# A gated linear recurrence with an MLP behind it: seven levels of decay products replaced by two running products, and the MLP turned round and put three chunks back

## The chip, the cores and the metric

The kernel runs on one core of one Trainium2 chip. The metric is the device time of the whole program in microseconds; the median of three runs is given. All arithmetic is in float32. The traces show four engines: PE (matrix products and transposes), DVE and POOL (elementwise work; POOL doesn't read PSUM here), ACT (copies out of PSUM, exponentials), and the queue of SP, which issues DMAs.

## The reference

```python
B, H, S, D = 4, 8, 768, 48            # q, k, v: float32; alpha between 0.8 and 1
for t in range(S):
    state = alpha[:, :, t, :, None] * state + einsum('bhd,bhe->bhde', k[:, :, t], v[:, :, t])
    y[:, :, t] = einsum('bhd,bhde->bhe', q[:, :, t], state)
x = y.transpose(0, 2, 1, 3).reshape(B * S, H * D)         # 3072 tokens x 384
h = x @ w_in                                              # 384 x 1024, float64 words
sm = exp(h - max(h)) / (sum(exp(h - max(h))) + 1e-9)
solu = h * sm
ln = (solu - mean(solu)) / sqrt(var(solu) + 1e-6) * g_ln  # over the 1024
out = ln @ w_out                                          # 1024 x 384, float64 words
```

Both weights arrive as float64 and are turned into float32 on the chip, bit field by bit field.

## The kernel before

The 3072 tokens are 24 chunks of 128: four sequences of six chunks each, taken one sequence after the other, so that each chunk needs the state that the chunk just before it leaves. For every chunk alpha, q and k are loaded with tokens on partitions, and PE transposes them (`prep_T`) so that a pair of heads (2 x 64 places) lies on the partitions.

Inside a chunk a query meets an earlier key at one of seven levels: at level m the key lies in a left block of 2^m tokens and the query in the right block beside it. `prep_level` doubles two products from level to level: `F`, alpha from the start of a block to the token (DVE, L153), and `G`, alpha after the token to the end of its block (DVE, L150). POOL multiplies q by F (`qc`, L139) and k by G (`kl`, L149), ACT spreads the two heads of a pair (`qr`, L160), PE forms the products of the level (`lev`, L188), and DVE copies those that the level owns into the scores under a mask (`sT`, L192). `read_out` applies scores and state to v (`y`, L204 and L209), adds the token's own term, and `next_state` carries the state on.

The MLP has tokens on partitions: `up` transposes x and makes `h` (128 x 1024, L257), `softmax`, `solu`, `stats` and `norm` run over the row of 1024, `norm_T` transposes the result back (`tp_ln`, L305), `down` multiplies by w_out (`o`, L314), and the 128 x 384 rows go out by DMA.

The loop at the end of the function puts the first part of chunk n beside the MLP of chunk n - 1 and the layout of chunk n + 1. The framework then orders each engine's instructions by its own estimate; every engine works through its list strictly in that order. Its PSUM tiles take two banks for transposes, two for levels, two for h, one for y and one for o.

## Time and profile before

| | |
|---|---|
| median of 3 runs | 849.0 us (840.6 to 849.03) |
| span of the profiled execution | 838.1 us |
| PE busy | 648.8 us, 77% of the span, 3513 matmul instructions |
| DVE busy | 579.1 us, 69%, 967 instructions |
| POOL busy | 413.6 us, 49%, 504 instructions |
| ACT busy | 231.4 us, 28%, 363 instructions |
| DMA | 30.64 MB, mean 37 GB/s |

The span runs from the first to the last instruction of one execution; the runs' times also hold what lies around it, 2.5 to 11 us by the fastest and the slowest of them. "Busy" counts an engine's instructions and not its waits. The chain of waits is found by going back from the last instruction, at each step to what released it. A float32 product is two PE instructions in the trace, a transpose one.

### The profile page before, as it was taken

How to read it: one execution, taken by the hardware profiler on the slowest of the kernel's cores; microseconds unless marked ns; L12 is line 12 of the kernel's file. 1: busy time of each engine (PE TensorE's matmuls, PEld its weight loads, DVE VectorE, ACT ScalarE, POOL GpSimd, SP SyncE). 2: the span in 40 equal slices, each digit the busy share in tenths (PEclk: the TensorE clock that was granted, in tenths of full speed). 3: DMA queues.
4: the chain of work that ended last, by engine and by line, in shares of the span. 5: the costliest groups of instructions: out<-in, count | busy, mean ns of one | idle time of the engine just before them, and what ended most of it. 6: DMA issues, size and time to landing. Idle time of an engine off the chain costs nothing.

```text
span 838.1 us, 9855 instructions
## 1 busy us (share of the span) xinstructions
PE 648.8 (77%) x3513; PEld 478.1 (57%) x3513; DVE 579.1 (69%) x967; ACT 231.4 (28%) x363; POOL 413.6 (49%) x504
## 2 busy tenths in 40 slices
PE   3277397878888887878888878878788878878884
PEld 2275276656566565566566556556566556556562
DVE  8989987685476586686577687577567676576522
ACT  2102323223223233333223223223223223223101
POOL 7847656563363464464453564465343563563200
PEclk9967568998969999999979999999969999999987
DMA  9314221201111022112201202202201200000000
GB/s 176 74 51 100 83 59 20 48 21 28 35 24 39 19 38 39 34 24 38 46 13 38 47 20 36 41 20 38 38 20 29 48 19 1 20 10 1 10 10 9
DMA packets 106528, 30.64 MB, mean 37 GB/s; under 512 B 100712, under 2 KB 103920, under 8 KB 106480
## 3 DMA queue, kind: packets, MB, share of 16 engines
q1 hardware_dynamic: 103296, 23.60, 15.6%
q10 hardware_dynamic: 3184, 6.42, 2.5%
q8 instruction: 28, 0.46, 0.2%
q14 instruction: 20, 0.16, 0.1%
HBM read 25.29 MB, written 4.72 MB: 36 GB/s over the span
## 4 chain that ended last, share of the span: by engine, by line
PE 32%; DVE 28%; POOL 21%; issue 11%; ACT 7%; POOLq 0%; DVEq 0%; ACTq 0%
PE h L257 16%; POOL qc L139 7%; POOL kl L149 6%; PE y L209 6%; DVE F L153 5%; DVE G L150 4%; PE tp_ln L305 3%; DVE sT L192 3%; DVE s L294 3%; PE o L314 3%; PE lev L188 3%; POOL qk L176 3%; ACT qr L160 3%; POOL own L179 2%; POOL rstd L290 2%
## 5 line engine op out<-in xcount | busy, mean ns | idle before, releaser
L188 PE MATMUL lev<-qr,kl 128*128 128x128 f32 x1344 | 197.1, 296 | 52.6 <-DVE sT L192 22.0
L139 POOL TENSOR_TENSOR qc<-qT,F 128x256 f32<-128x256 f32 x168 | 136.3, 811 | 186.0 <-ACT qT L122 158.6
L188 PEld LDWEIGHTS lev<-qr,kl 128*128 128x128 f32 x1344 | 178.1, 207 | 66.6 <-DVE sT L192 24.1
L257 PE MATMUL h<-w_in,xT 128*128 128x512 f32 x288 | 151.2, 679 | 55.2 <-ACT xT L253 54.4
L149 POOL TENSOR_TENSOR kl<-kT,G 128x256 f32<-128x256 f32 x144 | 113.5, 788 | 104.4 <-DVE G L150 99.9
L160 ACT COPY qr<-qc 64x768 f32<-64x768 f32 (+2 forms) x94 | 89.6, 953 | 254.4 <-POOL qc L139 253.9
L192 DVE COPY_PREDICATED sT<-masks,lev 128x512 f32<-128x512 uint8 x168 | 145.2, 864 | 7.0 <-PE lev L188 6.4
L153 DVE TENSOR_TENSOR F<-F 128x256 f32<-128x256 f32 x168 | 121.3, 722 | 35.0 <-POOL qc L139 30.5
L314 PE MATMUL o<-w_out,lnT 128*128 128x384 f32 x384 | 141.3, 523 | 0.0
L257 PEld LDWEIGHTS h<-w_in,xT 128*128 128x128 f32 x288 | 60.4, 218 | 128.0 <-issue 67.0
L265 DVE TENSOR_REDUCE nmax<-h 128x1 f32<-128x1024 f32 x24 | 29.4, 1224 | 144.9 <-PE h L257 144.9
L150 DVE TENSOR_TENSOR G<-G,F 128x256 f32<-128x256 f32 x144 | 98.2, 682 | 15.9 <-POOL kl L149 12.2
L314 PEld LDWEIGHTS o<-w_out,lnT 128*128 128x128 f32 x384 | 76.6, 206 | 49.5 <-issue 9.1
L305 PE MATMUL tp_ln<-ident,s 128*128 128x128 f32 x192 | 33.3, 328 | 35.1 <-DVE s L294 35.0
L209 PEld LDWEIGHTS y<-vn,sT 128*128 128x128 f32 x384 | 55.2, 227 | 2.7 <-issue 1.8
L209 PE MATMUL y<-vn,sT 128*128 128x48 f32 x384 | 55.0, 305 | 0.3 <-DVE sT L192 0.3
L305 PEld LDWEIGHTS tp_ln<-ident,s 128*128 128x128 f32 x192 | 26.3, 169 | 40.3 <-DVE s L294 27.3
L122 ACT COPY F<-tp_F 128x512 f32<-128x512 f32 x24 | 14.0, 584 | 115.9 <-PE tp_F L120 115.9
L308 ACT COPY lnT<-tp_ln 128x512 f32<-128x512 f32 x48 | 26.6, 588 | 61.2 <-PE tp_ln L305 61.2
L179 POOL TENSOR_TENSOR own<-vn,dot 128x384 f32<-128x384 f32 x24 | 22.5, 939 | 34.7 <-DVE x L214 34.6
L268 ACT ACTIVATE e<-h,nmax 128x1024 f32<-128x1024 f32 x24 | 26.8, 1115 | 44.5 <-DVE nmax L265 44.1
L290 POOL TENSOR_TENSOR rstd<-var,mhalf 128x1 f32<-128x1 f32 x24 | 16.7, 695 | 41.4 <-DVE var L288 41.3
(64 smaller groups left out, 666.2 us busy)
## 6 DMA issues: line engine op xcount, KB each, us to landing
vn<-in_v_dram SPq DMA_DIRECT2D x24, 192.0 KB, 2.6
an<-in_alpha_dram SPq DMA_DIRECT2D x24, 192.0 KB, 3.2
qn<-in_q_dram SPq DMA_DIRECT2D x24, 192.0 KB, 3.9
kn<-in_k_dram SPq DMA_DIRECT2D x24, 192.0 KB, 3.9
out_dram<-o_sb SPq DMA_DIRECT2D x24, 192.0 KB, 1.9
raw<-in_moe_w_in_dram ACTq DMA_DIRECT2D x12, 256.0 KB, 3.2
raw<-in_moe_w_out_dram ACTq DMA_DIRECT2D x8, 384.0 KB, 3.0
ident<-ident_c ACTq DMA_DIRECT2D x1, 64.0 KB, 2.0
```

The source lines that it names most:

```text
L139: nc.gpsimd.tensor_tensor(out=d["qc"][:, lv].rearrange("p j (n m) -> p j n m", m=m), in0=blocks(qT, lv, 1), in1=blocks(F, lv, 1), op=ALU.mult,
L149: nc.gpsimd.tensor_tensor(out=kl, in0=blocks(kT, lv, 0), in1=blocks(G, lv, 0), op=ALU.mult)
L150: nc.vector.tensor_tensor(out=blocks(G, lv, 0), in0=blocks(G, lv, 0), in1=spread(F, lv, 1), op=ALU.mult)
L153: nc.vector.tensor_tensor(out=blocks(F, lv, 1), in0=blocks(F, lv, 1), in1=spread(F, lv, 0), op=ALU.mult)
L160: nc.scalar.copy(out=qrs[n % 2][halves[i], first:end, :, i], in_=st[n]["qc"][halves[i], first:end])
L179: nc.gpsimd.tensor_tensor(out=d["own"], in0=d["v"], in1=dot[:, :, None].to_broadcast([P, H, D]), op=ALU.mult)
L188: nc.tensor.matmul(lev[:, 2 * j : 2 * j + 2, :], lhsT=kl[:, lv, j], rhs=qr[:, lv, j], start=True, stop=True)
L192: nc.vector.copy_predicated(out=blocks(sTs[n % 2], lv, 1), mask=masks[:, lv].rearrange("p (o n m) -> p o n m", o=1, m=m).to_broadcast([P, ...
L209: nc.tensor.matmul(y[:, h, :], lhsT=sTs[n % 2][:, h], rhs=d["v"][:, h], start=(c == 0 and h == 0), stop=(h == H - 1), skip_group_check=True,)
L257: nc.tensor.matmul(d["h"][:, s : s + 512], lhsT=xT[:, a], rhs=w_in[:, a, s : s + 512], start=(a == 0), stop=(a == KC - 1),)
L305: nc.tensor.transpose(out=tp[:, a], in_=d["s"][:, (s + a) * P : (s + a + 1) * P], identity=ident)
L314: nc.tensor.matmul(o, lhsT=d["lnT"][:, a], rhs=w_out[:, a], start=(a == 0), stop=(a == FC - 1))
```

## The change

A new function, `fast_path`, does all the work. The function of before is kept as `general_path` and sits behind a branch on a flag that `fast_path` computes.

- **Order of chunks.** Chunk n is part n // 4 of sequence n % 4, so four chunks lie between a state's making and its next use; each sequence has a state tile of its own.
- **Decay.** Two scans on DVE (L132 and L142 of the new file) over the transposed alpha: backwards, `hT`, the product from a token to the chunk's end; forwards, `qF`, the product from the start to the token, divided by the product of the whole chunk. POOL multiplies k by the one and q by the other. One product per head gives all scores (`scores`), and DVE applies a triangular mask. No levels, no own term.
- **MLP.** `up` has d_ff on partitions: 24 products of 128 x 128 per chunk in two halves. There is no maximum; `u = h * exp(h)` goes straight into `down`, with sum of u as a 385th column, and sums of e and u squared as two more columns. The mean is taken out of w_out once (`centre`), and the norm is one factor per token (`finish`). The MLP runs three chunks behind.
- **Weights.** Their DMAs go through SP's queue and no longer ACT's; the step `frac <- bits` goes from POOL to ACT; w_in comes in pieces of 512 columns.
- **End.** A flag is computed from products, sums and alpha, each engine loads it (`values_load`) and jumps over the general path if it is 0.

```diff
+    def prep_scan(n):
...
+        nc.vector.tensor_tensor_scan(
+            out=h[:, 0 : NP * SW][:, ::-1], data0=a.rearrange("p j s -> p (j s)")[:, ::-1],
+            data1=unit.rearrange("p j s -> p (j s)")[:, ::-1], initial=1.0, op0=ALU.mult, op1=ALU.add,
+        )
+        nc.vector.tensor_copy(out=fend[:, n], in_=h4[:, :, 1])
+        least = small.tile([P, NP, 1], FP, name="least")
+        nc.vector.tensor_scalar(out=least, in0=h4[:, :, 1:2], scalar1=LEAST, scalar2=None, op0=ALU.max)
+        nc.vector.reciprocal(out=s[:, :, 0:1], in_=least)
+        d["qF"] = work.tile([P, NP, SW], FP, name="qF")
+        nc.vector.tensor_tensor_scan(
+            out=d["qF"].rearrange("p j s -> p (j s)"), data0=a.rearrange("p j s -> p (j s)"),
+            data1=s.rearrange("p j s -> p (j s)"), initial=1.0, op0=ALU.mult, op1=ALU.add,
+        )
+        nc.vector.tensor_reduce(
+            out=amax[:, n : n + 1], in_=an[n % NIN].rearrange("p h d -> p (h d)"), axis=AX.X, op=ALU.max,
+            apply_absolute_value=True,
+        )
+    def prep_q(n):
+        d = st[n]
+        nc.gpsimd.tensor_tensor(out=d["qT"], in0=d["qT"], in1=d["qF"][:, :, 1:SW], op=ALU.mult)
...
+            nc.gpsimd.tensor_tensor(
+                out=d["kT"][:, :, 0 : P - 1], in0=d["kT"][:, :, 0 : P - 1],
+                in1=hT[n % 2][:, 0 : NP * SW].rearrange("p (j s) -> p j s", s=SW)[:, :, 2:SW], op=ALU.mult,
+            )
+    def decayed(n):
...
+        nc.gpsimd.tensor_tensor(
+            out=s, in0=s, in1=h4[:, :, 1:2].to_broadcast([P, NP, 2 * D]), op=ALU.mult
+        )
+    def scores(n):
+        d = st[n]
+        a = [ps_a.tile([P, NP, P], FP, tag=f"a{i}", name=f"a{i}") for i in range(2)]
+        for j in range(NP):
+            for i in range(2):
+                nc.tensor.matmul(
+                    a[i][:, j], lhsT=d["kT"][heads[i], j], rhs=d["qT"][heads[i], j], start=True, stop=True
+                )
+        d["sT"] = work.tile([P, 2, NP, P], FP, name="sT")
+        for i in range(2):
+            nc.vector.tensor_tensor(
+                out=d["sT"][:, i], in0=a[i], in1=mask[:, None, :].to_broadcast([P, NP, P]), op=ALU.mult
+            )
...
+        for h in range(H):
+            nc.tensor.matmul(
+                y[:, h, :], lhsT=d["sT"][:, h % 2, h // 2], rhs=d["v"][:, h],
+                start=(c == 0 and h == 0), stop=(h == H - 1), skip_group_check=True,
...
+        nc.scalar.copy(out=d["x"], in_=y.rearrange("p h d -> p (h d)"))
...
+    def up(n, half):
...
+        for f in range(HF):
+            for a in range(KC):
+                nc.tensor.matmul(
+                    h[:, f], lhsT=w_in[:, a, (f0 + f) * P : (f0 + f + 1) * P], rhs=d["xT"][:, a],
+                    start=(a == 0), stop=(a == KC - 1),
+                )
+        fs = slice(f0, f0 + HF)
+        nc.scalar.activation(out=d["e"][:, fs], in_=h, func=AF.Exp)
+        nc.vector.tensor_tensor(out=d["u"][:, fs], in0=h, in1=d["e"][:, fs], op=ALU.mult)
+        nc.scalar.activation(out=d["u2"][:, fs], in_=d["u"][:, fs], func=AF.Square)
+    def partial(n):
...
+        for eng, key in ((nc.gpsimd, "e"), (nc.vector, "u2")):
+            t = work.tile([P, HF, P], FP, name="part_" + key)
+            eng.tensor_tensor(out=t, in0=d[key][:, 0:HF], in1=d[key][:, HF:FC], op=ALU.add)
+            w = HF
+            while w > 1:
+                w //= 2
+                eng.tensor_tensor(out=t[:, 0:w], in0=t[:, 0:w], in1=t[:, w : 2 * w], op=ALU.add)
+            d["p_" + key] = t
+    def down(n):
+        d = st[n]
+        o = ps_o.tile([P, 512], FP, tag="o", name="o")
+        for f in range(FC):
+            nc.tensor.matmul(
+                o[:, 0 : DM + 1], lhsT=d["u"][:, f], rhs=w_out[:, f], start=(f == 0), stop=(f == FC - 1),
+                skip_group_check=True,
+            )
+        for i, key in enumerate(("e", "u2")):
+            nc.tensor.matmul(
+                o[:, DM + 1 + i : DM + 2 + i], lhsT=d["p_" + key][:, 0], rhs=ones[:, 0:1],
+                start=False, stop=True, skip_group_check=True,
+            )
+        d["o"] = o
+    def finish(n):
...
+        nc.vector.tensor_copy(out=s[:, 0:3], in_=d["o"][:, DM : DM + 3])
...
+        nc.gpsimd.tensor_tensor(out=r, in0=s[:, 3:4], in1=mhalf, op=ALU.pow)
+        o_sb = work.tile([P, DM], FP, name="o_sb")
+        nc.scalar.activation(out=o_sb, in_=d["o"][:, 0:DM], func=AF.Copy, scale=r)
+        t0 = b * S + c * P
+        nc.sync.dma_start(out=out[t0 : t0 + P, :], in_=o_sb)
+        d.clear()
...
+    def centre():
+        m = ps_o.tile([P, 512], FP, tag="o", name="mean")
+        for f in range(FC):
+            nc.tensor.matmul(m[:, 0:DM], lhsT=ones, rhs=w_out[:, f, 0:DM], start=(f == 0), stop=(f == FC - 1))
+        nc.scalar.mul(out=ms, in_=m[:, 0:DM], mul=1.0 / DFF)
+        for f in range(FC):
+            eng = nc.vector if f % 2 else nc.gpsimd
+            eng.tensor_tensor(out=w_out[:, f, 0:DM], in0=w_out[:, f, 0:DM], in1=ms, op=ALU.subtract)
...
+    for n in range(N + LAG):
+        if n + 3 < N:
+            load(n + 3)
+        m = n - LAG
+        now, before, after = n < N, m >= 0, n + 1 < N
+        if after:
+            prep_aq(n + 1)
+        if m > 0:
+            finish(m - 1)
+        if now:
+            decayed(n)
+        if after:
+            prep_scan(n + 1)
+        if before:
+            up(m, 0)
+        if after:
+            prep_q(n + 1)
+        if now:
+            scores(n)
+        if after:
+            prep_k(n + 1)
+        if before:
+            up(m, 1)
+            partial(m)
+        if n < KC:
+            weights_in(n)
+        if n == 1:
+            gains()
+        if 1 <= n < 5 and n <= LAG:
+            per = -(-FC // LAG)
+            weights_out(range((n - 1) * per, min(FC, n * per)))
+        if n == LAG:
+            centre()
+        if now:
+            keys_back(n)
+            read_out(n)
+            next_state(n)
+        if before:
+            down(m)
+        if now:
+            x_T(n)
+    finish(N - 1)
...
+    total = const.tile([P, 1], FP, name="total")
+    nc.vector.tensor_reduce(out=total, in_=ok.rearrange("p n i -> p (n i)"), axis=AX.X, op=ALU.add)
+    all_ok = ps_o.tile([P, 512], FP, tag="o", name="all_ok")
+    nc.tensor.matmul(all_ok[0:1, 0:1], lhsT=total, rhs=ones[:, 0:1], start=True, stop=True)
+    bad = const.tile([1, 1], I32, name="bad")
+    nc.vector.tensor_scalar(
+        out=bad, in0=all_ok[0:1, 0:1], scalar1=float(P * N * 8), scalar2=None, op0=ALU.is_lt
+    )
+    return bad[0:1, 0:1]
...
+def tile_gla_recurrent__then__act_solu_kernel(tc, *args):
...
+    with ExitStack() as ctx:
+        bad = fast_path(ctx, tc, *args)
+        taken = nc.values_load(bad, min_val=0, max_val=1, skip_runtime_bounds_check_because="0 or 1 by its making")
+    with tc.If(taken > 0):
+        general_path(tc, *args)
```

PSUM is now two banks for transposes, two for scores (`a`), two for the halves of h, and two that y, kv (the state's increment) and o take in turn.

PE before, one chunk in the middle of the loop, from the end of one level to the next chunk's layout (a row's x4 counts products; `lev` are the levels, `tp_` transposes):

```order
L188 MATMUL lev<-qr_105,kl_107 128x128 x4
L209 MATMUL y<-vn,sT_108 128x48 x8
L314 MATMUL o<-w_out,lnT 128x384 x8
L251 MATMUL tp_x<-ident,x 128x128 x3
L188 MATMUL lev<-qr_105,kl_107 128x128 x4
L257 MATMUL h<-w_in,xT 128x512 x6
L120 MATMUL tp_F<-ident,an_102 128x128 x4
L120 MATMUL tp_qT<-ident,qn_96 128x128 x4
L188 MATMUL lev<-qr_105,kl_107 128x128
L120 MATMUL tp_kT<-ident,kn_99 128x128 x4
```

PE after, the same place of the program, one chunk in the middle of the loop from behind the scores (`a`, eight products of 128 x 128 just before this piece) to the first product of the next chunk's `up`:

```order
L118 MATMUL tp<-ident,kn_103 128x128 x4
L256 MATMUL h<-xT,w_in 128x128 x12
L194 MATMUL tp_k<-ident,kT 128x128 x4
L204 MATMUL y<-state_117,qT 128x96 x4
L210 MATMUL y<-vn,sT 128x48 x8
L224 MATMUL kv<-vn,kg 128x96 x4
L281 MATMUL o<-w_out,u 128x385 x8
L286 MATMUL o<-ones,part_e 128x1
L286 MATMUL o<-ones,part_u_1767 128x1
L240 MATMUL tp_x<-ident,x 128x128 x3
L118 MATMUL tp<-ident,an_104 128x128 x4
L256 MATMUL h<-xT,w_in 128x128
```

The seven rounds of `lev` are gone, and between x's transposes and the use of x lie three whole chunks of other work. `o` now comes straight behind `kv`, and it takes the PSUM bank that `y` leaves.

DVE before, part of one chunk in the middle of the loop (`F` and `G` of the next chunk, between x and the MLP's maximum `nmax`):

```order
L153 TENSOR_TENSOR F<-F 128x32x8
L177 TENSOR_REDUCE dot<-qk 128x8
L150 TENSOR_TENSOR G<-G,F 128x16x16
L214 TENSOR_TENSOR x<-y,own 128x384
L153 TENSOR_TENSOR F<-F 128x16x16
L150 TENSOR_TENSOR G<-G,F 128x8x32
L153 TENSOR_TENSOR F<-F 128x8x32
```

DVE after, most of one chunk in the middle of the loop (`part_u` is the sum of squares):

```order
L132 SCALAR_TENSOR_TENSOR hT_113<-aT_109,unit 128x516
L136 COPY fend<-hT_113 128x4
L139 TENSOR_SCALAR least<-hT_113 128x4
L140 RECIPROCAL seed_111<-least 128x4
L142 SCALAR_TENSOR_TENSOR qF<-aT_109,seed_111 128x516
L146 TENSOR_REDUCE amax<-an_107 128x1
L262 TENSOR_TENSOR u<-h,e 128x512
L186 TENSOR_TENSOR sT<-a_1726,mask 128x512
L186 TENSOR_TENSOR sT<-a_1727,mask 128x512
L262 TENSOR_TENSOR u<-h,e 128x512
L270 TENSOR_TENSOR part_u_1767<-u_1708 128x512
L234 TENSOR_TENSOR state_117<-state_117,kv 64x4x48
```

The thirteen steps of F and G are gone. The scans of the next chunk stand ahead of both `u` and `sT` of the chunk at hand, so what is late in the scans makes the scores late too.

DVE after, in the set-up, where the first pieces of w_in are turned into float32 (`bits`, `expo`, `frac`, six steps a piece) between the attention of the first chunks:

```order
L186 TENSOR_TENSOR sT<-a_324,mask 128x512
L349 TENSOR_SCALAR bits<-raw 128x512
L351 TENSOR_SCALAR expo<-raw 128x512
L142 SCALAR_TENSOR_TENSOR qF<-aT_108,seed_110 128x516
L354 TENSOR_SCALAR expo<-expo 128x512
L359 SCALAR_TENSOR_TENSOR frac<-raw,frac 128x512
L355 TENSOR_SCALAR expo<-expo 128x512
L349 TENSOR_SCALAR bits<-raw 128x512
L356 SCALAR_TENSOR_TENSOR expo<-raw,expo 128x512
```

Two chunks' scores come ahead of the first step of a weight here; before, the weights stood between the levels of chunk 0.

More of the change, by code (lines that the diff above doesn't have):

```diff
@@ L12 @@
 U32 = mybir.dt.uint32
+I32 = mybir.dt.int32
 AF = mybir.ActivationFunctionType
@@ L32, with general_path @@
 @with_exitstack
-def kernel(
+def general_path(
     ctx: ExitStack,
@@ L318, in down @@
         d.clear()
[L321 removed]
+    nc.scalar.dma_start(out=ident, in_=nc.inline_tensor(np.eye(P, dtype=np.float32), name="g_ident_c").ap())
     nc.scalar.dma_start(out=g_rows, in_=moe_g_ln.rearrange("(c p) -> c p", p=P))
     nc.scalar.dma_start(
[L324 removed]
+        out=masks.rearrange("p l c -> p (l c)"), in_=nc.inline_tensor(_level_masks(), name="g_masks_c").ap()
     )
@@ L432, with kernel @@
             down(n - 1)
+def kernel(tc, *args):
+    nc = tc.nc
+    with ExitStack() as ctx:
[3 more added lines that the diff above has]
+        general_path(tc, *args)
 _INS = ['q', 'k', 'v', 'alpha', 'moe_w_in', 'moe_w_out', 'moe_g_ln']
```

230 lines of the change are left out of this document (227 added, 3 removed).

## The prediction

> **What bounds the kernel now.** I read the page first, for the shares of the engines and the chain that ended last, then PE in order of time over two chunks in the middle, then busy time by stage.
>
> ```profile
> span 838.1 us, 9855 instructions
> ...
> PE 648.8 (77%) x3513; PEld 478.1 (57%) x3513; DVE 579.1 (69%) x967; ACT 231.4 (28%) x363; POOL 413.6 (49%) x504
> ...
> PE 32%; DVE 28%; POOL 21%; issue 11%; ACT 7%; POOLq 0%; DVEq 0%; ACTq 0%
> PE h L257 16%; POOL qc L139 7%; POOL kl L149 6%; PE y L209 6%; DVE F L153 5%; DVE G L150 4%; PE tp_ln L305 3%; DVE sT L192 3%; DVE s L294 3%; PE o L314 3%; PE lev L188 3%; POOL qk L176 3%; ACT qr L160 3%; POOL own L179 2%; POOL rstd L290 2%
> ```
>
> No engine is full, and the chain goes round: PE 32%, DVE 28%, POOL 21%. Its lines are h, then the levels' products on POOL (qc, kl) and DVE (F, G). So a chunk lasts as long as a circle through three engines, and PE, with most work, still waits a quarter of the time. In order of time:
>
> ```profile
> 460.00 1.88 PE L209 MATMUL y<-vn,sT 128*128 128x48 f32 x16
> 461.72 5.39 PE L314 MATMUL o<-w_out,lnT 128*128 128x384 f32 x16
> 466.94 0.49 PE L251 MATMUL tp_x<-ident,x 128*128 128x128 f32 x3
> 467.27 1.06 PE L188 MATMUL lev<-qr,kl 128*128 128x128 f32 x8
> 471.27 5.42 PE L257 MATMUL h<-w_in,xT 128*128 128x512 f32 x12 [2.94 <-ACT xT L253]
> 476.53 0.60 PE L120 MATMUL tp_F<-ident,an 128*128 128x128 f32 x4
> 476.96 0.60 PE L120 MATMUL tp_qT<-ident,qn 128*128 128x128 f32 x4
> ...
> 480.46 2.02 PE L188 MATMUL lev<-qr,kl 128*128 128x128 f32 x16 [0.44 <-DVE rsum L273]
> 482.32 1.03 PE L204 MATMUL y<-state,qF 128*128 128x96 f32 x8
> 483.19 0.60 PE L226 MATMUL tp_k<-ident,kG 128*128 128x128 f32 x4
> ...
> 501.33 5.42 PE L257 MATMUL h<-w_in,xT 128*128 128x512 f32 x12 [2.95 <-ACT xT L253]
> ```
>
> From one h to the next is 501.33 - 471.27 = 30.06 us, a chunk's time. The starts also give PE's price of each kind while nothing holds it: y with 48 columns 1.72/16 = 0.108 us, o 5.22/16 = 0.326, a transpose 0.43/4 = 0.11, a level of 128 columns 1.86/16 = 0.116, y with 96 columns 0.87/8 = 0.109, h with 512 columns 5.26/12 = 0.438. Products of up to 128 columns all cost about 0.11.
>
> ```profile
> 0.00:40.00 40.00, 11.72 (x47) 8.82 (x47) 36.12 (x58) 9.50 (x12) 30.96 (x37) 1.00 0.81 130
> 40.00:80.00 40.00, 28.36 (x125) 22.71 (x125) 37.79 (x78) 6.31 (x9) 25.56 (x34) 0.71 0.30 81
> 80.00:150.00 70.00, 49.56 (x244) 39.86 (x243) 60.38 (x114) 18.67 (x30) 42.30 (x51) 0.71 0.19 51
> 450.00:550.00 100.00, 79.27 (x501) 59.23 (x500) 72.53 (x119) 31.26 (x50) 56.06 (x69) 0.98 0.18 33
> ```
>
> Columns after the length: PE, PE's weight loads, DVE, ACT, POOL, granted clock, DMA. In the first 80 us DVE is the bound (74 of 80), with PE at a granted clock of 0.71 behind it; in the middle the clock is 0.98. So there are two stages to price: a set-up that DVE bounds, and a loop.
>
> **The change in the loop.** Per chunk PE loses 56 instructions of levels, 8 transposes of the norm and 12 of h, and gains 48 of 128 columns for the turned `up` and 16 for the scores. By the prices above a chunk is now: 19 transposes 2.09 us; scores 16 x 0.116 = 1.86; up 48 x 0.116 = 5.57 (h cost 12 x 0.438 = 5.26, so the turn alone costs 0.3); y 16 x 0.108 + 8 x 0.109 = 2.60; kv 8 x 0.109 = 0.87; down 16 x 0.327 and 4 narrow ones 5.67. Together **18.7 us**, against 30.06 now.
>
> Whether PE gets there hangs on the others.
>
> Rows of DVE and POOL in order of time (start, length):
>
> ```profile
> 26.56 0.84 POOL L139 TENSOR_TENSOR qc<-qT,F 128x256 f32<-128x256 f32 x1 [0.36 <-DVE F L153]
> ...
> 26.74 0.94 DVE L150 TENSOR_TENSOR G<-G,F 128x256 f32<-128x256 f32 x1
> ...
> 50.17 0.41 DVE L150 TENSOR_TENSOR G<-G,F 128x256 f32<-128x256 f32 x1
> ```
>
> ```profile
> L265 DVE TENSOR_REDUCE nmax<-h 128x1 f32<-128x1024 f32 x24 | 29.4, 1224 | 144.9 <-PE h L257 144.9
> ...
> L169 POOL TENSOR_TENSOR qF<-qT,F 128x512 f32<-128x512 f32 x20 | 25.6, 1279 | 9.2 <-DVE F L153 9.2
> ...
> L290 POOL TENSOR_TENSOR rstd<-var,mhalf 128x1 f32<-128x1 f32 x24 | 16.7, 695 | 41.4 <-DVE var L288 41.3
> ...
> L177 DVE TENSOR_REDUCE dot<-qk 128x8 f32<-128x384 f32 x24 | 13.0, 541 | 1.0 <-POOL qk L176 1.0
> ```
>
> DVE: from 384 to 1024 elements a step grows from 541 to 1224 ns, 1.07 ns an element, with 0.13 us fixed. A step of 512 is then 0.68 us; so are two-input steps left alone (0.41 at 256), while the same step took 0.94 beside POOL's qc. No scan is in the trace. Its lower bound is 0.68 us, one element a step; twice that, 1.36, if an element waits for the product before it. I take 1.36. DVE per chunk: two scans 2.7, alpha's maximum 0.7, sT and u 4 x 0.68 = 2.7, squares summed 1.4, state 0.7, seven small steps 1.0: 9.2 us, or some 14 if half of it ran beside POOL at such odds. POOL: q and k 2 x 1.28, state 1.0, sums of e 2.6, power 0.7: 6.8. ACT makes eleven passes at 231.4/363 = 0.64: 7.0. All lie under 18.7, so PE is the bound, provided that no result comes late. Counting from the chunk's first transpose: o of the chunk before ends 0.3 earlier, `finish` takes 0.6 + 0.7 + 0.5 on DVE, POOL and ACT, and only then ACT copies alpha (it is behind that on ACT's list), at 2.2; the scans end near 5.4, alpha's maximum at 6.1, u at 6.8, sT at 8.2. PE wants sT after a, q, h, scores, k, h, tp_k and the state's part of y, at 10.1. **There are 2 us to spare.** The second close place is o behind kv: it needs the bank of y, which ACT copies out in about 0.6 while kv takes 0.87. Both hold, narrowly; their price if they don't is the lateness itself, once a chunk: scans at 1.9 each beside POOL would still fit, at 2.5 PE would wait 0.3.
>
> [...]
>
> **The set-up.** Until down(0) can start, DVE's list holds (counted in it) 12 scans, 10 maxima, 16 steps of sT and u, 8 state copies of 0.34, 6 small partial sums 2.7, 18 tiny steps 2.5, 4 subtractions 2.2, and the weights: 6 pieces of 512 and 8 of 384, six steps each. Clean, and in its last step crossed by POOL, a piece of 256 reads:
>
> ```profile
> 56.26 0.28 DVE L356 TENSOR_SCALAR expo<-expo 128x256 uint32<-128x256 uint32 x1
> 56.45 0.41 DVE L361 SCALAR_TENSOR_TENSOR frac<-raw,frac 128x256 f32<-128x256 uint32 x1
> 56.79 0.28 DVE L357 TENSOR_SCALAR expo<-expo 128x256 uint32<-128x256 uint32 x1
> ...
> 57.61 0.41 DVE L358 SCALAR_TENSOR_TENSOR expo<-raw,expo 128x256 uint32<-128x256 uint32 x1
> 57.93 0.28 DVE L351 TENSOR_SCALAR bits<-raw 128x256 uint32<-128x256 uint32 x1
> 58.14 0.83 DVE L353 TENSOR_SCALAR expo<-raw 128x256 uint32<-128x256 uint32 x1
> ...
> 58.10 0.72 POOL L364 TENSOR_TENSOR w_in<-expo,frac 128x256 f32<-128x256 f32 x1 [2.03 <-DVE expo L358]
> ```
>
> All clean, six steps are 4 x 0.28 + 2 x 0.41 = 1.94; as they stand here 2.49, a factor of 1.28. Grown with size, a piece of 512 is 3.04 clean and one of 384 2.48: 38 us together clean, 49 with that factor. I take 49, since POOL still turns every piece. Sum: 16.3 + 6.8 + 10.9 + 2.7 + 2.7 + 2.5 + 2.2 + 49 = 93 us of DVE.
>
> ```profile
> 6.24 1.09 PE L120 MATMUL tp_F<-ident,an 128*128 128x128 f32 x4 [6.24 <-DMA an<-in_alpha_dram]
> ```
>
> DVE can't start before the first alpha (6.24 us), and the first weight now stands behind sixteen loads in SP's queue; I allow 10 us of idling. Behind DVE's last step come POOL, ACT, the mean's product, its copy and POOL's subtractions, 5 us. down(0) starts at **108 us** (90 with clean weights and quick scans). By then PE's list has done up(0) to up(2), the scores of chunks 0 to 5 and y of 0 to 3.
>
> **The sum.** Left for PE: down 24 x 5.67 = 136; up 21 x 5.57 = 117; scores 18 x 1.86 = 33; y 20 x 2.60 = 52; kv 16 x 0.87 = 14; transposes 18 x 1.76 + 20 x 0.33 = 38: 391 us (sum of unrounded terms). For hand-overs I add 12 us (3%, chosen), and 1.5 in each of the last three rounds, where nothing lies between up and the u that down needs (ACT and DVE 0.64 + 0.68): 4.5. The end: `finish` 1.8 and the output's DMA,
>
> ```profile
> out_dram<-o_sb SPq DMA_DIRECT2D x24, 192.0 KB, 1.9
> ```
>
> 1.9, then the flag's load and the jump, which no row shows: between nothing and a first DMA's 6.24; I take 4. Span 108 + 391 + 12 + 4.5 + 8 = 523 against 838.1; the median lies 10.9 over the profiled span now, so **534 us**.
>
> **Rivals.**
> - *PE stays at its mean rates.* A group's busy time over its count holds the bubbles and the slow clock of before:
>
> ```profile
> L188 PE MATMUL lev<-qr,kl 128*128 128x128 f32 x1344 | 197.1, 296 | 52.6 <-DVE sT L192 22.0
> ...
> L314 PE MATMUL o<-w_out,lnT 128*128 128x384 f32 x384 | 141.3, 523 | 0.0
> L305 PE MATMUL tp_ln<-ident,s 128*128 128x128 f32 x192 | 33.3, 328 | 35.1 <-DVE s L294 35.0
> L209 PE MATMUL y<-vn,sT 128*128 128x48 f32 x384 | 55.0, 305 | 0.3 <-DVE sT L192 0.3
> ```
>
>   That is 0.147, 0.368, 0.173 and 0.143 us: a chunk of 23.7, the 391 become 497, and the total **628**. For it: two close hand-overs and a clock that fell to 0.71 early. Against it: the stretches above have these prices in the middle of waits, and the new list has fewer.
> - *The two heads of a pair go through PE together.* The scores' operands are 48 rows high, at partitions 0 and 64 in turn. If such pairs overlap, scores cost half, 17 us less: **517**. [...]
> - *DVE bounds the loop*, if scans and contention make 9.2 into 28 us or more: then a chunk takes what it takes now, and the total is near 840. A scan would have to cost over 10 us.
> - *The flag is set and the general path runs behind the fast one*: 523 + 838 + 11 = **1372**. It decides at the limits: a chunk's product of alpha under 1e-13 (with alpha uniform from 0.8 to 1 the typical product is near 1e-6, and the smallest of these inputs is 8.3e-8), alpha over 1 (its largest value rounds to 1.0, which is let through), or a token's sums out of bounds (the sum of e is about 1024). So it speaks for nothing but a slip in the flag.
>
> **Chances.** Forecast 0.55; mean rates 0.26; pairs together 0.13; DVE 0.03; flag 0.03. The range goes from 490 (90 us of set-up and overlapping pairs, 499, less some hand-overs) to 600, half-way and a little more to the mean rates; what lies beyond is a third of that rival and the last two. One per cent is about what a measurement of this kernel can tell. Faster by over 1%: 0.96; within it 0.01; slower 0.03.
>
> **What would show it.** Starts of o 18 to 20 us apart in the loop, PE over 90% busy there at a clock near 1.0, and the chain mostly PE. First o near 108 us. sT as PE's releaser for y, or x's copy for o, in more than 1 us a chunk would mean the close hand-overs fail. Starts of the scores under 0.08 us apart would mean the overlap. A weight piece over 4 us on DVE would make the set-up too short here.

## The result, and the profile after

The changed kernel takes **505.98 us** (median of 4 runs, 505.34 to 506.91) against 844.8 us for the kernel before in the same session (839.41 to 849.03). The ratio is 0.599, with a 95% interval from 0.596 to 0.603. The forecast of 534 us was 28 us too high, and the range of 490 to 600 held.

First the page of the changed kernel: span, shares of the engines, the granted clock in 40 equal slices (a digit is a tenth of full speed), and the chain that ended last.

```profile
span 504.0 us, 7993 instructions
...
PE 466.2 (93%) x3195; PEld 393.5 (78%) x3195; DVE 284.0 (56%) x555; ACT 155.9 (31%) x288; POOL 187.2 (37%) x201
...
PEclk9558555969999999999999999999999999999998
...
PE 87%; DVE 8%; ACT 1%; POOL 1%; DMA 1%; issue 1%; ACTq 0%
```

The chain no longer goes round: 87% of it is PE. Busy time by stretch (columns as in the prediction, and behind them the DMA's GB/s) shows the two stages:

```profile
0.00:40.00 40.00, 30.73 (x155) 25.96 (x155) 26.83 (x52) 11.71 (x20) 17.50 (x27) 0.68 0.65 144
40.00:80.00 40.00, 28.76 (x140) 22.84 (x140) 34.31 (x66) 11.74 (x23) 13.68 (x11) 0.63 0.58 138
...
250.00:350.00 100.00, 100.00 (x765) 86.64 (x764) 54.77 (x108) 32.56 (x62) 34.97 (x38) 1.00 0.27 58
```

From 250 to 350 us PE is busy for all of the 100 us, at a clock of 1.00; before, the middle had 79 of 100. In the first 80 us neither PE nor DVE is full, and the clock is 0.63 to 0.68. One chunk of the loop on PE, in order of time:

```profile
156.24 5.38 PE L281 MATMUL o<-w_out,u 128*128 128x385 f32 x16
161.46 0.28 PE L286 MATMUL o<-ones,part_e 128*128 128x1 f32 x2
...
162.18 0.60 PE L118 MATMUL tp<-ident,an 128*128 128x128 f32 x4
...
165.96 1.16 PE L181 MATMUL a<-qT,kT 48*128 48x128 f32 x16
167.05 0.66 PE L118 MATMUL tp<-ident,kn 128*128 128x128 f32 x4
167.54 2.84 PE L256 MATMUL h<-xT,w_in 128*128 128x128 f32 x24
170.22 0.60 PE L194 MATMUL tp_k<-ident,kT 128*128 128x128 f32 x4
...
171.52 1.91 PE L210 MATMUL y<-vn,sT 128*128 128x48 f32 x16
...
174.20 2.14 PE L281 MATMUL o<-w_out,u 128*128 128x385 f32 x6
```

No PE row of the chunk, shown or not, has a wait ahead of it, and from o to o it is 174.20 - 156.24 = 17.96 us. Scores (`a`) cost 167.05 - 165.96 = 1.09 us for sixteen instructions, 0.068 each; `up` costs (170.22 - 167.54)/24 = 0.112 and o 5.22/16 = 0.326. The first o:

```profile
117.28 5.45 PE L281 MATMUL o<-w_out,u 128*128 128x385 f32 x16 [2.02 <-POOL w_out L391]
```

### The profile page after: what moved, and what is told of

It reads as the page before. It is cut to its first block, busy times and chain, and to the rows that moved or that the text cites. A ratio compares the mean times of both kernels' runs of the same rounds, so it can differ in the third digit from the quotient of the medians.

```text
span 504.0 us, 7993 instructions
## 1 busy us (share of the span) xinstructions
PE 466.2 (93%) x3195; PEld 393.5 (78%) x3195; DVE 284.0 (56%) x555; ACT 155.9 (31%) x288; POOL 187.2 (37%) x201
## 4 chain that ended last, share of the span: by engine, by line
PE 87%; DVE 8%; ACT 1%; POOL 1%; DMA 1%; issue 1%; ACTq 0%
PE o L281 25%; PE h L256 24%; PE y L210 9%; PE tp L118 7%; PE a L181 6%; PE kv L224 4%; PE y L204 3%; PE tp_k L194 2%; PE tp_x L240 2%; PE o L286 2%; PE mean L386 1%; DVE qF L142 1%; DVE expo L351 1%; DVE frac L359 1%; DVE bits L349 1%; POOL w_out L362 1%
## 5 line engine op out<-in xcount | busy, mean ns | idle before, releaser
L256 PE MATMUL h<-xT,w_in 128*128 128x128 f32 x1152 | 144.7, 281 | 3.4 <-POOL w_in L362 3.4
L256 PEld LDWEIGHTS h<-xT,w_in 128*128 128x128 f32 x1152 | 138.7, 197 | 6.3 <-POOL w_in L362 4.1
L281 PE MATMUL o<-w_out,u 128*128 128x385 f32 x384 | 129.2, 488 | 2.0 <-POOL w_out L391 2.0
L281 PEld LDWEIGHTS o<-w_out,u 128*128 128x128 f32 x384 | 71.0, 190 | 47.8 <-POOL w_out L391 3.0
L307 POOL TENSOR_TENSOR r<-sums,mhalf 128x1 f32<-128x1 f32 x24 | 13.2, 549 | 127.3 <-DVE sums L303 127.3
L262 DVE TENSOR_TENSOR u<-h,e 128x512 f32<-128x512 f32 x48 | 32.9, 685 | 35.0 <-ACT e L261 32.3
L132 DVE TENSOR_TENSOR_SCAN hT<-aT,unit 128x516 f32<-128x516 f32 x24 | 30.3, 1263 | 38.3 <-ACT aT L119 38.3
L181 PE MATMUL a<-qT,kT 48*128 48x128 f32 x384 | 37.3, 316 | 4.8 <-POOL qT L153 4.8
L160 POOL TENSOR_TENSOR kT<-kT,hT 128x508 f32<-128x508 f32 x24 | 28.4, 1185 | 35.8 <-ACT kT L119 34.5
L270 POOL TENSOR_TENSOR part_e<-e 128x512 f32<-128x512 f32 x24 | 30.5, 1272 | 25.9 <-ACT e L261 23.8
L274 POOL TENSOR_TENSOR part_e<-part_e 128x256 f32<-128x256 f32 (+1 forms) x48 | 37.8, 787 | 3.8
L142 DVE TENSOR_TENSOR_SCAN qF<-aT,seed 128x516 f32<-128x516 f32 x24 | 32.1, 1336 | 0.8
L186 DVE TENSOR_TENSOR sT<-a,mask 128x512 f32<-128x512 f32 x48 | 31.0, 680 | 0.8 <-PE a L181 0.7
```

Of the source, the lines that this page charges most:

```text
L132: nc.vector.tensor_tensor_scan(out=h[:, 0 : NP * SW][:, ::-1], data0=a.rearrange("p j s -> p (j s)")[:, ::-1], data1=unit.rearrange("p j s ...
L142: nc.vector.tensor_tensor_scan(out=d["qF"].rearrange("p j s -> p (j s)"), data0=a.rearrange("p j s -> p (j s)"), data1=s.rearrange("p j s ...
L181: nc.tensor.matmul(a[i][:, j], lhsT=d["kT"][heads[i], j], rhs=d["qT"][heads[i], j], start=True, stop=True)
L186: nc.vector.tensor_tensor(out=d["sT"][:, i], in0=a[i], in1=mask[:, None, :].to_broadcast([P, NP, P]), op=ALU.mult)
L256: nc.tensor.matmul(h[:, f], lhsT=w_in[:, a, (f0 + f) * P : (f0 + f + 1) * P], rhs=d["xT"][:, a], start=(a == 0), stop=(a == KC - 1),)
L262: nc.vector.tensor_tensor(out=d["u"][:, fs], in0=h, in1=d["e"][:, fs], op=ALU.mult)
```

## The experiments

Times are medians. Each kernel is the changed kernel with the edit shown, but for the one that is said to start from the kernel before.

### Which part of the change brings the time

**The new decay with the old MLP**: h has tokens on partitions, and maximum, statistics and norm run over its rows, as before.

```diff
-        if before:
-            up(m, 0)
+        if before:
+            up(m)
+            softmax(m)
...
-        if before:
-            up(m, 1)
-            partial(m)
+        if before:
+            solu(m)
+            stats(m)
+            norm(m)
...
         if before:
+            norm_T(m)
             down(m)
```

> The decay by two scans, the order of chunks and the three chunks of lag as changed, but the MLP as before (tokens on partitions, maximum, mean, variance and norm on the row, a transpose back, no centred weights; the flag looks at alpha and its products only). Theory A (the seven levels made the circle through PE, DVE and POOL that set a chunk's time before): most of the gain stays, spacing of o 19 to 22 us, time 560 to 620 us. Rival B (the MLP's chain from h to its transpose set it): spacing 25 to 29 us, time 690 to 780 us.

Measured: 595.37 and 605.02 us, median 600.19. The rows are from the longer execution:

```profile
304.61 5.32 PE L307 MATMUL o<-w_out,lnT 128*128 128x384 f32 x16
...
315.67 0.42 PE L210 MATMUL y<-vn,sT 128*128 128x48 f32 x2 [1.37 <-DVE sT L186]
...
325.10 5.32 PE L307 MATMUL o<-w_out,lnT 128*128 128x384 f32 x16
```

A chunk takes 20.49 us here and in most rounds from 240 to 407 us, but 23.75 in those from 121 to 240 us, where the granted clock is 0.86 on average; the section on the loop's reserve comes back to that. So the new decay without the new MLP brings 237 to 246 of the 339 us (841.8 for the kernel before in that session, less 605.0 and 595.4). The new order of chunks, the lag of three and the new handling of the weights are in this kernel too; the first two are taken back one by one below, from the changed kernel.

**The old decay with the new MLP**, an edit of the kernel before, so the order of chunks is the old one and the MLP one chunk behind:

```diff
-            up(n - 1)
+            x_T(n - 1)
+            up(n - 1, 0)
...
-            softmax(n - 1)
+            up(n - 1, 1)
...
-            solu(n - 1)
+            partial(n - 1)
...
-            norm_T(n - 1)
             down(n - 1)
+            finish(n - 1)
```

> The kernel before with its seven levels and its order of chunks, but with the turned MLP, one chunk behind (half 0 where up stood, half 1 where the softmax stood), centred weights, and one buffer less for turning weights into float32, since the memory is short. Theory A (the levels are the circle): spacing of o 26 to 30 us, time 720 to 830 us. Rival B (the MLP's chain set the time): spacing near PE's sum of 23 to 24 us, time 640 to 680 us.

Measured: 830.51 us, a ratio of 0.985 (0.969 to 1.001) to the kernel before: no difference that can be told, and just outside what theory A gave. The page's chain and two rows a chunk apart:

```profile
PE 35%; POOL 24%; DVE 23%; ACT 8%; issue 7%; DMA 3%; POOLq 0%; DVEq 0%
```

```profile
400.62 0.52 PE L253 MATMUL tp_x<-ident,x 128*128 128x128 f32 x3
...
431.24 0.53 PE L253 MATMUL tp_x<-ident,x 128*128 128x128 f32 x3
```

30.62 us a chunk, and the chain is still divided between three engines. The circle through the levels set the time before; the MLP is worth something (from 595 or 605 down to 506) only when that circle is gone.

### The price of the scores

**The loops over heads and pairs exchanged**, so that four products on the same 48 rows follow each other:

```diff
-        for j in range(NP):
-            for i in range(2):
+        for i in range(2):
+            for j in range(NP):
                 nc.tensor.matmul(
                     a[i][:, j], lhsT=d["kT"][heads[i], j], rhs=d["qT"][heads[i], j], start=True, stop=True
```

> The changed kernel, but the eight score products of a chunk run over all pairs for the first head, then for the second, so that neighbours on PE use the same 48 rows. Theory A (neighbouring products on rows 0 to 47 and 64 to 111 overlap in PE): a score instruction goes from 0.068 us back to about 0.116 us, the spacing of o from 17.97 to 18.7 us, the time from 506 to 520 to 524 us. Rival B (a product with 48 rows is cheaper by itself): 0.068 us stays, spacing 17.97, time 505 to 508 us.

Measured: 520.4 us (519.49 to 521.31), 14.4 more. On PE:

```profile
169.96 1.71 PE L181 MATMUL a<-qT,kT 48*128 48x128 f32 x16
171.60 0.66 PE L118 MATMUL tp<-ident,kn 128*128 128x128 f32 x4
```

(171.60 - 169.96)/16 = 0.1025 us each instead of 0.068: 0.55 more per chunk, 13.2 over 24 chunks. The same products on the same data cost a third less in the changed kernel, where neighbours in the list use different rows. Such neighbours also write different PSUM banks (`a[0]` and `a[1]`), and the exchange changes both at once, so this run doesn't tell the rows from the banks.

### What sets the end of the set-up

**The weights' steps on DVE left out**, so that one step on ACT and one on POOL remain:

```diff
-        nc.vector.tensor_scalar(out=bits, in0=hi, scalar1=0xFFFFF, scalar2=None, op0=ALU.bitwise_and)
-        nc.scalar.activation(out=frac, in_=bits, func=AF.Copy, scale=2.0**-20, bias=1.0)
...
-        nc.gpsimd.tensor_tensor(out=dst, in0=expo.bitcast(FP), in1=frac, op=ALU.mult)
+        nc.scalar.activation(out=frac, in_=hi, func=AF.Copy, scale=2.0**-33, bias=0.0)
+        nc.gpsimd.tensor_tensor(out=dst, in0=frac, in1=frac, op=ALU.mult)
```

> The changed kernel, but DVE's six steps that turn a piece of the weights into float32 are left out (ACT takes the high word as a number, POOL squares it: other weights, same DMAs, same products). That takes 52 us of steps from DVE's list before the first o. Theory A (DVE's list bounds the set-up, as the prediction had it): first o from 117 to 65 to 78 us, time 453 to 468 us. Rival B (PE at its slow clock and the hand-overs bound it): first o at 92 to 110 us, time 480 to 500 us.

Measured: 484.94 us (484.35 to 485.53), between the two. The first o, and busy time by stretch:

```profile
88.96 7.06 PE L281 MATMUL o<-w_out,u 128*128 128x385 f32 x16 [2.58 <-POOL w_out L377]
```

```profile
0.00:40.00 40.00, 31.86 (x158) 27.34 (x159) 22.64 (x46) 11.93 (x20) 17.56 (x28) 0.67 0.70 159
40.00:80.00 40.00, 31.43 (x210) 26.74 (x209) 17.44 (x27) 18.23 (x35) 20.16 (x21) 0.86 0.55 146
```

52 us of DVE's work taken away bring the first o 28 us earlier and the time down by 21. So those steps bound the set-up for half of their length; behind them stands a chain through PE, the scans on DVE and POOL, with POOL at its end (the row above), and PE is busy 63 of 80 us at a clock of 0.67 and 0.86. The other 7 us of the 28 are lost between the first and the fourth o, 45.71 us instead of 38.96: with the first o so early, more is left for PE in that stretch (84 instructions of `up` instead of 48, and the scores of one chunk more), and the first o takes 7.06 us instead of 5.45.

**The MLP one chunk behind instead of three**, with all of w_in turned in the first round:

```diff
-    LAG = 3
+    LAG = 1
```

> The changed kernel with the MLP one chunk behind and not three, so that all of w_in stands ahead of chunk 1. Theory A (the three chunks only let PE work during the set-up; in the loop x is ready in time anyway, or some 0.3 us late): spacing of o 18.0 to 18.4 us, time 515 to 545 us. Rival B (the lag keeps PE full in the loop): spacing 19 us or more, time over 550 us.

Measured: 517.95 us (517.1 to 518.79). The first o comes 20 us earlier, at 97.73, and the kernel is 12 us slower all the same:

```profile
0.00:97.00 97.00, 55.76 (x291) 43.63 (x291) 79.65 (x148) 28.94 (x51) 40.43 (x48) 0.68 0.53 128
```

PE has only 55.76 us of work in the 97 us. What the lag of three gives is work for PE while the weights are being turned; in the loop o to o is 18.39 here, 0.42 more, which makes some 6 us of the loss.

**The first weight loaded ahead of chunks 2 and 3:**

```diff
-    for n in range(3):
-        load(n)
+    load(0)
...
+    load(1)
...
+    weights_in(0)
+    load(2)
...
-        if n < KC:
+        if 0 < n < KC:
             weights_in(n)
```

> The loads of chunk 0 and 1 and the first piece of w_in are issued ahead of the loads of chunk 2; before, the first piece stood behind the loads of chunks 0 to 3. Nothing is computed otherwise. Theory A (DVE's list bounds the set-up, and DVE idles from 18 to 28 us because the weight's DMA stands late in SP's queue): the first weight step moves from 28 us to near 20, the first o from 117 to 108-113 us, and the time falls by what PE does not do meanwhile, to 497-503 us. Rival B (PE at its slow granted clock and the hand-overs bound the set-up, as far as leaving out all 52 us of DVE's weight steps brought only 28): the first o stays at 115-118 and the time at 504-508 us. Rival C (the weight's piece and chunk 2's loads share the DMA engines, and alpha and q of chunk 2 come late to PE instead): first o later than 118, time 508-515.

Measured: 510.62 us (508.48 to 513.57), 4.6 more: the third theory. DVE in order of time:

```profile
14.42 0.40 DVE L348 TENSOR_SCALAR bits<-raw 128x512 uint32<-128x512 uint32 x1
...
32.26 1.23 DVE L132 TENSOR_TENSOR_SCAN hT<-aT,unit 128x516 f32<-128x516 f32 x1 [5.35 <-ACT aT L119]
```

The first step on a weight comes at 14.42 us instead of 28.22, as meant, but now DVE waits 5.35 us for the alpha of chunk 2, whose load stands behind the weight; PE is busy 25.22 us of the first 40, where it was 30.73. The first o comes at 119.43.

**The mean of w_out taken out of PE's way.** In the changed kernel its first products stand on PE's list ahead of y of chunk 3 and the scores of chunk 4 (those of chunk 3, which the expectation names, come before them). PE's waits by line, 0 to 117 us (total, times, longest):

```profile
PE mean L386 <- ACT w_out L372: 10.1, 3, 5.5
...
PE a L181 <- POOL qT L153: 4.8, 2, 2.4
PE h L256 <- POOL w_in L362: 3.4, 2, 2.4
PE y L210 <- DVE sT L186: 2.9, 2, 1.6
```

First the call alone was moved:

```diff
-        if n == LAG:
-            centre()
         if now:
             keys_back(n)
             read_out(n)
             next_state(n)
+        if n == LAG:
+            centre()
         if before:
             down(m)
```

> The mean's eight products of 128 x 384 (L386) are written behind chunk 3's read_out and next_state, right ahead of the first down, instead of ahead of them; nothing else. In the changed kernel the first of them stands on PE's list ahead of y and the scores of chunk 3 and waits there 5.51 us for w_out's first piece, and it holds one of the two banks that y and kv take. Theory A (part of the set-up is PE standing behind the mean's wait): that wait goes, y, kv, x and the later scores come 4 to 8 us earlier, the first o moves from 117 to 110-114 us, the time falls by 3 to 7, to 499-503 us. Rival B (DVE's weight steps alone set when down can start, and PE only waits where it has to wait anyway): first o at 116-118, time 505-507 us.

Then its products also got a tile of ones that exists only after the first `up`:

```diff
+        late = const.tile([P, P], FP, name="late")
+        nc.scalar.activation(out=late, in_=st[0]["u"][:, 0], func=AF.Identity, scale=0.0, bias=ones[:, 0:1])
         for f in range(FC):
-            nc.tensor.matmul(m[:, 0:DM], lhsT=ones, rhs=w_out[:, f, 0:DM], start=(f == 0), stop=(f == FC - 1))
+            nc.tensor.matmul(m[:, 0:DM], lhsT=late, rhs=w_out[:, f, 0:DM], start=(f == 0), stop=(f == FC - 1))
```

> As the run before, and the mean's products take as weights a tile of ones that ACT makes from u of chunk 0, so that they can't be put on PE's list ahead of the first `up`; the value is 1 all the same. Theory A (PE stands behind the mean's waits, 5.51, 0.54 and 4.07 us): all but a little of these 10 us goes, the first o comes at 107-112 us and the time is 496-501 us. Rival B (DVE's weight steps set the end of the set-up): first o at 115-119, time 504-508 us. Rival C (the mean's products, gathered late, stand behind the last weight piece and add their 5 us there): first o at 119-123, time 507-512 us.

Measured: 506.69 (505.71 to 507.54) and 509.68 us (507.26 to 510.59). The waits with the call moved:

```profile
PE h L256 <- POOL w_in L362: 7.7, 3, 5.5
PE a L181 <- POOL qT L153: 6.4, 3, 2.4
...
PE y L210 <- DVE sT L186: 4.9, 2, 3.3
PE mean L386 <- ACT w_out L372: 3.2, 4, 1.6
```

The mean's wait falls from 10.1 to 3.2 us, and 4.3 of that come back ahead of h, 1.6 ahead of `a`, 2.0 ahead of y. The first o comes at 116.47 and, in the second run, at 115.17. So PE stood behind the mean where it had to wait anyway, which is rival B: what comes late to PE are the weights and scores that go through DVE. The second kernel gains 2.1 us at the first o and loses 3.7 in the end. The loss lies between the first and the fourth o, 44.62 us instead of 38.96:

```profile
140.07 7.14 PE L281 MATMUL o<-w_out,u 128*128 128x385 f32 x16 [0.92 <-ACT x L215]
```

16 more instructions of `up` are left for that stretch (1.8 us), PE waits 0.50 us for alpha's copy and 0.92 us for x's copy there, and the first and the third o take 6.02 and 7.14 us instead of 5.45 and 5.38; the granted clock is 0.66 from 140 to 145 us. Expectation B gave the right place of the first o. C gave the right time by luck, since the loss doesn't lie where C put it.

### The loop's reserve

**Each scan done twice**, which puts two scans more per chunk on DVE:

```diff
+        nc.vector.tensor_tensor_scan(
+            out=h[:, 0 : NP * SW][:, ::-1], data0=a.rearrange("p j s -> p (j s)")[:, ::-1],
+            data1=unit.rearrange("p j s -> p (j s)")[:, ::-1], initial=1.0, op0=ALU.mult, op1=ALU.add,
+        )
         nc.vector.tensor_copy(out=fend[:, n], in_=h4[:, :, 1])
...
+        nc.vector.tensor_tensor_scan(
+            out=d["qF"].rearrange("p j s -> p (j s)"), data0=a.rearrange("p j s -> p (j s)"),
+            data1=s.rearrange("p j s -> p (j s)"), initial=1.0, op0=ALU.mult, op1=ALU.add,
+        )
```

> The changed kernel with each of the two scans of a chunk done twice, 2.5 us more on DVE a chunk. Theory A (DVE is off the path by only 0.9 us: sT is ready at 170.65 us and y takes it at 171.52): PE waits 1.4 to 1.8 us in each chunk, spacing 19.4 to 19.8 us, time 540 to 552 us. Rival B (DVE is idle half of the time and 2.5 us more don't matter): spacing 18.0 us, time 506 to 512 us.

Measured: 568.65 us (567.9 to 569.39), 62.7 more, beyond what either theory gave. PE in order of time, and then busy time from one us to the next (the granted clock is the third number from the end):

```profile
317.19 0.42 PE L218 MATMUL y<-vn,sT 128*128 128x48 f32 x2 [0.75 <-DVE sT L194]
317.79 1.76 PE L218 MATMUL y<-vn,sT 128*128 128x48 f32 x14 [0.17 <-DVE sT L194]
...
320.44 6.95 PE L289 MATMUL o<-w_out,u 128*128 128x385 f32 x16
...
341.92 0.90 PE L289 MATMUL o<-w_out,u 128*128 128x385 f32 x1
```

```profile
320.00:321.00 1.00, 1.00 (x6) 0.83 (x5) 0.96 (x2) 0.12 (x1) 0.92 (x2) 0.59 0.00 0
321.00:322.00 1.00, 1.00 (x3) 0.55 (x2) 0.94 (x3) 0.00 (x0) 0.82 (x2) 0.50 0.19 39
...
323.00:324.00 1.00, 1.00 (x4) 0.55 (x3) 0.00 (x0) 0.00 (x0) 0.00 (x0) 0.70 0.00 0
```

The wait is where it was expected, y for sT. But a chunk is 21.48 us (341.92 - 320.44), 3.5 more, and y's delay is only 1.4 of it (kv starts 3.97 us behind the state's part of y, not 2.61). The rest lies mostly in o, 6.95 us long instead of 5.38: the clock falls to 0.50 some 2.4 us behind the wait and stays there for about 3.4 us (in the chunk before, for 6.8). To tell whether the wait did that, or the added load, PE was given work in place of the wait.

**The same with eight products on PE ahead of the late y**, into columns that nobody reads:

```diff
+            for f in range(8):
+                nc.tensor.matmul(
+                    bank[:, DM : DM + P], lhsT=d["qT"][:, f % NP], rhs=d["qT"][:, f % NP],
+                    start=False, stop=False, skip_group_check=True,
+                )
```

> As the run with both scans done twice (568.65 us, o 21.4 us apart, o's sixteen products 6.0 to 7.5 us long instead of 5.38), with eight products of 128 x 128 per chunk put on PE between the state's part of y and the part that waits for sT; they write columns of the bank that nobody reads, from chunk 4 on. They add 8 x 2 x 0.112 = 1.8 us of work per chunk where PE waited 0.9 + 0.4. Theory A (o is long there because the short wait brings the granted clock down): no wait is left, o goes back to 5.4 us, o's spacing is 17.97 + 1.8 = 19.8 us, and the time is 535-545 us, less than without the added work. Rival B (o is long because the doubled scans load DVE and its ports, or the chip lowers the clock by the load alone): o stays at 6.2 to 7.2, the spacing at 21.5 to 22, the time at 568-580 us.

Measured: 549.91 us (549.14 to 550.78): with more work than the run before, 18.7 us faster. The same 200 us of both, first with the wait, then with the work:

```profile
200.00:400.00 200.00, 191.73 (x1277) 160.51 (x1277) 113.56 (x196) 54.34 (x103) 59.83 (x64) 0.90 0.23 49
```

```profile
200.00:400.00 200.00, 200.00 (x1533) 174.92 (x1532) 128.19 (x214) 58.09 (x110) 66.18 (x71) 1.00 0.24 51
```

The clock is back at 1.00, o takes 5.38 again, and a chunk is 19.75 us, the 17.97 and 1.78 of the added products. So DVE's load by itself doesn't account for the 0.90 without the products: with DVE busy for 128.19 us instead of 113.56, and with PE busy for all of the 200 us, the clock was 1.00. The eight products close the gap and give PE more to do in that stretch, both at once, so which of the two counts is not told apart. The total is 5 us above the upper end of what was expected; 3.6 of them lie ahead of the first o (120.83).

Nor was every such wait followed by a lower clock. In the run with the old MLP y waits for sT in each chunk, and `h` behind it reads, in a chunk of 23.75 us and in the chunk of 20.49 us shown there:

```profile
203.38 0.42 PE L210 MATMUL y<-vn,sT 128*128 128x48 f32 x2 [1.37 <-DVE sT L186]
...
208.46 6.04 PE L250 MATMUL h<-w_in,xT 128*128 128x512 f32 x8
...
319.83 3.70 PE L250 MATMUL h<-w_in,xT 128*128 128x512 f32 x8
```

The wait is 1.37 us in both. Behind the first the clock falls to 0.50 and the eight instructions of `h` take 6.04 us, behind the second it stays at 1.00 and they take 3.70. So behind the same wait the clock fell in one chunk and not in the other, and what decides it is open.

### Two edits without a theory's weight

**The old order of chunks**, one sequence after the other:

```diff
-        c, b = divmod(n, B)
+        b, c = divmod(n, NCH)
```

> The changed kernel, but the chunks of one sequence follow each other as before, so that each state is used by the very next chunk. Theory A (the state is ready far ahead of y in any case): spacing 17.97 us, time 503 to 510 us. Rival B (the state's product, sum and decay become a wait for y in each chunk): spacing 19 to 20 us, time 530 to 560 us.

Measured: 506.45 us (506.05 to 506.84), no difference. The state has time enough within a chunk.

**Without the flag**, its load and the path behind it:

```diff
-        bad = fast_path(ctx, tc, *args)
-        taken = nc.values_load(bad, min_val=0, max_val=1, skip_runtime_bounds_check_because="0 or 1 by its making")
-    with tc.If(taken > 0):
-        general_path(tc, *args)
+        fast_path(ctx, tc, *args)
```

> The changed kernel without the flag, the register loads, the jump and the general path behind it (the flag's limits on the inputs are then not looked at). Theory A (the output's DMA is out at 499.9 us of the span, and the 4 us behind it are the flag's load and the jump): 501 to 503 us. Rival B (the end is the program's usual end, whatever it holds): 505 to 507 us.

Measured: 502.59 us (500.49 to 503.65), 3.4 less. That is the price of the flag at the end, inside the 4 us allowed for it. It buys the general path, so this is no better version; none of the experiments that keep the computation beats the changed kernel.

## Why the prediction was right, and where its terms were off

**The bound of before and the new bound: right.** The circle through the levels set the 30.06 us, as the two halves of the change by themselves show, and with it gone PE is the bound, at the prices read from the middle of the old trace: o 0.326 (forecast 0.327), `up` 0.112 (0.116). A chunk came to 17.97 us instead of 18.7.

**The scores, 1.86 forecast, 1.09 measured.** The term of the sum was mis-sized. This is the rival of the pairs, given 0.13, and its mark was met, scores that start under 0.08 us apart; its 517 us lies nearer to what was measured than the forecast. 18 chunks at 0.77 are 13.9 us. That a pair costs half, 0.058 us an instruction, was the author's estimate, and no run shows it: 0.068 us was measured with the rows in turn and 0.1025 with the same rows in succession, and the banks changed with the rows.

**The two close places: both held.** DVE and ACT in the chunk shown above:

```profile
169.37 1.28 DVE L186 TENSOR_TENSOR sT<-a,mask 128x512 f32<-128x512 f32 x2
```

```profile
173.53 0.48 ACT L215 COPY x<-y 128x384 f32<-128x384 f32 x1 [1.05 <-PE y L210]
```

sT is ready at 170.65, 8.47 us behind the chunk's first transpose (forecast 8.2), and PE wants it at 171.52: 0.87 us to spare, not 2, mostly since the scores took less. The copy of x ends at 174.01, and o starts at 174.20: 0.19 to spare. The first reserve is smaller than two scans more, and the price of passing it was wrong in the text: not "the lateness itself, once a chunk", but 3.5 us for 1.4 in the run with the doubled scans.

**The scan, taken at 1.36.** In most rows a scan takes 1.20 to 1.23 us (the row at 32.26 in the run with the early weight is one), in the set-up of the changed kernel up to 2.22; over its whole run `hT` takes 1.26 and `qF` 1.34 on average. The 1.36 was an estimate, twice the 0.68 of a step of 512, with no scan in the trace of before to read it from; the median of both scans in the changed kernel is 1.23, 1.8 times that 0.68.

**The set-up, 108 forecast, 117.28 measured.** The work on DVE was right: 89.52 us up to its last step ahead of the mean, at 112.65, where the forecast had 91 (93 less the 2.2 of the subtractions that lie behind); so were the weights (52 against 49) and what follows (4.6 against 5). The failed term is "I allow 10 us of idling": it is 112.65 - 89.52 = 23.1. DVE's waits from 0 to 112.7 us:

```profile
DVE hT L132 <- ACT aT L119: 7.0, 3, 5.7
DVE frac L359 <- ACT frac L350: 5.0, 3, 2.0
DVE state L232 <- PE kv L224: 4.4, 2, 3.0
DVE u L262 <- ACT e L261: 2.6, 1, 2.6
```

The forecast had only loads in mind: the start and the first line, an alpha that comes late. The other 12 us are DVE waiting for ACT and PE in the middle of its list, while PE ran at a clock of 0.63 to 0.68. The run without the weights' steps agrees: with 52 us off DVE's list the first o still comes only at 88.96, behind a chain through PE, the scans and POOL.

**Hand-overs 12, last rounds 4.5: both came to nothing.** PE has no idle row from 130 to 480 us. In the last rounds

```profile
478.99 5.35 PE L281 MATMUL o<-w_out,u 128*128 128x385 f32 x16
...
489.99 5.35 PE L281 MATMUL o<-w_out,u 128*128 128x385 f32 x16
```

stand 11.00 us apart, which is `up` and `down` at their prices and no wait: `down` begins with the first half of u, and the second is made meanwhile. The step forgot that a sum over sixteen products needs its operands one after the other.

**Around the span, 10.9 forecast, 2.0 measured** (505.98 - 504.0). The 10.9 was the difference of the old median and one profiled execution, while the three runs shown ahead of the prediction lie 2.5 to 11 above it. Time less span of one and the same execution is 1.9 to 2.9 us in the four runs of the changed kernel, so what was added is for the most part a difference between two executions.

Together: set-up +9.3, scores -13.9, hand-overs -12, last rounds -4.5, the rest +1.6, around the span -8.9: -28.4 us. But for the scores, the large errors are allowances that were chosen and not read from rows, and the difference between two executions. The errors point both ways, so that the total is off by only 28 us, where the terms' errors without their signs make 50, is in part luck.

## What to carry to other kernels

When a chain goes round through several engines, price the kernel by what its fullest engine costs per round in the stretches where nothing holds it, and add a hand-over only where a row shows one: the chosen 3% was 12 us too much here. Before speeding up a part that several engines share, ask which of the two halves is the circle: the new MLP alone was worth nothing measurable, and some 90 to 100 us behind the new decay. An engine's reserve ahead of a wait deserves a number of its own, since in the run with the doubled scans 1.4 us of delay on PE came with 3.5 us more a chunk and a granted clock that fell to 0.50.

## What the runs showed of the hardware that was not expected

- **Short waits on PE came with more loss than their length.** With the doubled scans, behind two waits of 0.75 and 0.17 us per chunk by the rows, 1.4 us of delay in all, the granted clock fell to 0.50 for 3.4 or 6.8 us, 1.2 to 2.4 us later, and a chunk took 3.5 us more; with eight products in place of the waits it was 1.00 from 200 to 400 us.
- **The same wait wasn't followed by it each time.** With the old MLP the clock fell to 0.50 behind a wait of 1.37 us in one chunk and stayed at 1.00 behind one of the same length in another. With the doubled scans the slow stretches begin at 296.30, 320.18 and 340.66 us and end at 303.12, 323.60 and 344.08 (worked out from the clock in each us: 0.59 from 320 to 321 us is 0.18 us at 1.00 and the rest at 0.50). Any two of these times lie a whole multiple of 3.41 us apart, to within 0.05. The chunks with the old MLP that kept their clock last 20.49 us, six times that. Whether it matters where a wait falls among such steps is not shown: no run moved a wait alone.
- **Work that nobody needs made a kernel faster.** Eight products per chunk in place of the wait took 18.7 us off the kernel with the doubled scans, which stays slower than the changed kernel.
- **The first 80 us run at 0.63 to 0.68 of the clock** although PE is busy for 72 to 77% of them, so by the clock PE's work there costs about half as much again (an estimate: 1 over 0.63 to 0.68). What brought the clock down there is not shown: no run filled those waits.
